# Retention attention feeding a Mish MLP on one core: first tile's chunks interleaved, four DMA transposes moved to TensorE, loads and stores reordered

## The chip, the core and the metric

The kernel runs on one core of a Trainium2 chip. A core has TensorE (PE in the profile; its weight loads are PEld), VectorE (DVE), ScalarE (ACT), GpSimd (POOL), a queue that only issues transfers (SP), and 16 DMA engines that all queues share. Each engine takes its instructions in program order and waits at the first one that is not ready. The metric is the device time of one execution in microseconds (us); lower is better.

## The reference, cut to what matters

```python
# q, k, v: (8 batches, 8 heads, 576 positions, 64), f32
scores = (1 / sqrt(64)) * q @ k^T
Dmat   = gamma[h] ** (i - j) where i >= j, else 0      # gamma = 1 - 2**(-5-h)
ret    = (scores * Dmat) @ v
x      = ret as (4608, 512)                            # 8 * 576 tokens, 8 heads * 64
h      = x @ w_in                                      # (512, 2048)
g      = h * tanh(softplus(h))                         # Mish
out    = g @ w_out                                     # (2048, 512), f32
```

## The kernel before

**Work units.** The 576 positions of a batch are cut into four chunks of 128 and one of 64; the two short ones of a pair of batches are put together. That makes 36 chunks of 128 tokens. Four chunks make a tile, so there are nine tiles, numbered t = 0 to 8. Chunks 0 to 3 are tile 0, chunks 4 to 7 tile 1, chunk 8 (a joined one) begins tile 2.

**Attention of a chunk n** has four steps, written P, T, S, O:

- P (`prep`, lines 160 to 168): DVE scales q by the decay and the softmax scale into bf16 (`qks`, line 166), GpSimd casts k (line 165) and scales v (`vs`, line 167).
- T (`step_t`, lines 170 to 181): q and k of the chunk are transposed into `qkT`, eight blocks of 128x128. For chunks 0 to 3 TensorE does it into PSUM and ACT copies it out (lines 177, 178); for all later chunks one DMA transpose on the ACT queue does it (line 180).
- S (`step_s`, lines 183 to 206): scores (`sc`, line 190), masked by DVE into `sm` (line 194), and the update of the running state k^T v (`st`, line 204).
- O (`step_o`, lines 208 to 231): state times q (line 218) and scores times v (line 223) into `ot`; DVE makes the next state copy `ssb` (line 227) and writes the chunk's columns of `xT` (line 231).

**The MLP.** `g1(t, f)` is four matmuls of 512 columns for one of 16 blocks f of the hidden width, and a Mish on ACT (line 244). `g2(t, i)` is four matmuls of the second product (line 252). Tile 0 is special: its second product is a loop over f (lines 317 to 331, "the f loop") with four accumulators, two of them in the pool of `hp`, and the attention of chunks 4 to 7 stands between its steps. Then four result tiles are copied and stored (line 333, `store` at lines 257 to 265; `res` has three buffers, so the fourth copy waits until the first store has left). Then t = 1 runs `g1(1, f)` with the attention of chunks 8 to 11 and the transposes of 9 to 12 in between and no second product; from t = 2 on each step has a `g1` and a `g2`.

**Order.** Nothing reorders instructions: the program's order is each engine's order. SP issues all loads and stores. Input buffers hold eight chunks (`io`, 8 buffers), `qks` and `vs` three, the score PSUM `sc` one. Weights come in eight pieces each through four staging buffers and are cast by GpSimd (lines 113, 115).

Of the kernel before, what the change touches and what calls it, by code (L numbers as in the profile page):

```python
# [10 lines left out]
F32 = mybir.dt.float32  # L11
BF16 = mybir.dt.bfloat16
AX = mybir.ActivationFunctionType
# [4 lines left out]
def kernel(  # L18
# [18 lines left out]
    nc = tc.nc  # L37
    B, H, S, D = q.shape
    assert (B, H, S, D) == (8, 8, 576, 64)
    P = 128  # L40
    NP = H // 2
# [4 lines left out]
    NCH = 4  # L46
# [10 lines left out]
    consts = ctx.enter_context(tc.tile_pool(name="consts", bufs=1))  # L57
# [7 lines left out]
    STG = 4  # L65
    stage = ctx.enter_context(tc.tile_pool(name="stage", bufs=STG))
    PS = bass.MemoryType.PSUM
    ps_sc = ctx.enter_context(tc.tile_pool(name="ps_sc", bufs=1, space=PS))
# [3 lines left out]
    ps_o = ctx.enter_context(tc.tile_pool(name="ps_o", bufs=2, space=PS))  # L72
# [6 lines left out]
    def load(n):  # L79
        b, c = chunks[n]  # L80
        tiles = []
        for nm, src in (("q", q), ("k", k), ("v", v)):
            t = io.tile([P, H, D], F32, name=f"{nm}raw")
            if c < 4:
                nc.sync.dma_start(  # L85
                    out=t, in_=src[b, :, ds(P * c, P), :].rearrange("h p d -> p h d"))
            else:
                for e in range(2):
                    nc.sync.dma_start(
                        out=t[ds(64 * e, 64)],  # L90
                        in_=src[b + e, :, ds(512, 64), :].rearrange("h p d -> p h d"))
            tiles.append(t)
        raw[n] = tiles
# [8 lines left out]
    def load_w(nm, i):  # L102
        t = stage.tile([P, 1024], F32, name="wst")
        if nm == "in":
            nc.sync.dma_start(out=t.rearrange("p (c f) -> p c f", c=KC), in_=w_in_r[:, :, ts(i, 256)])  # L105
        else:
            nc.sync.dma_start(out=t.rearrange("p (f d) -> p f d", f=2), in_=w_out_r[:, ts(i, 2), :])
        staged[nm, i] = t

    def cast_w(nm, i):  # L110
        t = staged.pop((nm, i))
        if nm == "in":
            nc.gpsimd.tensor_copy(w_in_t[:, :, ts(i, 256)], t.rearrange("p (c f) -> p c f", c=KC))  # L113
        else:
            nc.gpsimd.tensor_copy(w_out_t[:, ts(i, 2), :], t.rearrange("p (f d) -> p f d", f=2))
# [20 lines left out]
    gv = consts.tile([P, 5, H], F32)  # L136
    nc.scalar.activation(gq, ex, AX.Exp)
    nc.scalar.activation(gv, ex, AX.Exp, scale=-1.0)
    nc.vector.tensor_scalar(gq, gq, 1.0 / math.sqrt(D), None, op0=OP.mult)

    mask = consts.tile([P, P], F32)
# [18 lines left out]
    def prep(n):  # L160
        b, c = chunks[n]
        qr, kr, vr = raw.pop(n)
        qks = tok.tile([P, 2, H, D], BF16, name="qks")
        vs = tok.tile([P, H, D], BF16, name="vs")
        nc.gpsimd.tensor_copy(qks[:, 1], kr)  # L165
        nc.vector.tensor_tensor(qks[:, 0], qr, gq[:, c, :].unsqueeze(2).to_broadcast([P, H, D]), op=OP.mult)  # L166
        nc.gpsimd.tensor_tensor(vs, vr, gv[:, c, :].unsqueeze(2).to_broadcast([P, H, D]), op=OP.mult)  # L167
        live[n] = (qks, vs)

    def step_t(n):  # L170
        qks, vs = live[n]
        flat = qks.rearrange("p i h d -> p (i h d)")
        qk = tr.tile([P, 2, NP, P], BF16, name="qkT")
        if n < NCH:
            tp = ps_o.tile([P, 2 * NP, P], BF16, name="ops")
            for i in range(2 * NP):
                nc.tensor.transpose(tp[:, i, :], flat[:, ts(i, P)], ident)  # L177
            nc.scalar.copy(qk.rearrange("p i n t -> p (i n) t"), tp)
        else:
            nc.scalar.dma_start_transpose(out=qk.rearrange("p i n t -> p (i n) t"), in_=flat)  # L180
        live[n] = (qk, qks[:, 1], vs)

    def step_s(n):
        b, c = chunks[n]
        qk, ks, vs = live[n]
        sc = ps_sc.tile([P, 2, NP, P], F32, name="sc")
        for p in range(NP):
            for e in range(2):
                r = ds(64 * e, 64)
                nc.tensor.matmul(sc[:, e, p, :], lhsT=qk[r, 1, p, :], rhs=qk[r, 0, p, :],  # L190
                                 start=True, stop=True)
        sm = tr.tile([P, 2, NP, P], BF16, name="sm")
        m = mask if c < 4 else mask2
        nc.vector.tensor_tensor(  # L194
            sm.rearrange("p e n i -> p (e n) i"), sc.rearrange("p e n i -> p (e n) i"),
            m.unsqueeze(1).to_broadcast([P, 2 * NP, P]), op=OP.mult)
        if c < 4:
            if c == 0:
                st_ps[b] = ps_st.tile([P, NP, P], F32, name="st")
            st = st_ps[b]  # L200
            kf = ks.rearrange("p h d -> p (h d)")
            vf = vs.rearrange("p h d -> p (h d)")
            for p in range(NP):
                nc.tensor.matmul(st[:, p, :], lhsT=kf[:, ts(p, P)], rhs=vf[:, ts(p, P)],  # L204
                                 start=(c == 0 and p == 0), stop=True, skip_group_check=True)
        live[n] = (qk, sm, vs)
# [60 lines left out]

    n_chunks = len(chunks)

    def att(n, step):  # L270
        if n >= n_chunks:
            return
        if step == "P":
            prep(n)
            if n >= 2 * NCH - 1 and n + PF < n_chunks:
                load(n + PF)
        elif step == "T":
            step_t(n)
        elif step == "S":
            step_s(n)  # L280
        else:
            step_o(n)


    for n in range(NCH):
        for step in "PTSO":
            att(n, step)
    for i in range(8):
        cast_w("in", i)
        if i + STG < 8:  # L290
            load_w("in", i + STG)
        g1(0, 2 * i)
        g1(0, 2 * i + 1)
    load(4)
    att(4, "P")
    att(4, "T")
    for i in range(STG):
        load_w("out", i)
        if i % 2:
            load(4 + (i + 1) // 2)  # L300

    accs = [ps_o.tile([P, d_model], F32, name="ops") for _ in range(2)]
    accs += [ps_h.tile([P, NCH * P], F32, name="hp") for _ in range(2)]

    def more(j, n):
        cast_w("out", j)
        if j + STG < 8:
            load_w("out", j + STG)
        if j == 1:
            load(7)  # L310
        elif j == 3:
            for m in range(2 * NCH, 2 * NCH + 4):
                load(m)
        elif j in (4, 6):
            load(2 * NCH + 2 + j // 2)

    for f in range(nF):
        n, w = NCH + f // 4, f % 4
        if w == 0:
            more(f // 2, n)  # L320
            att(n, "S")
        elif w == 1:
            att(n + 1, "P")
        elif w == 2:
            more(f // 2, n)
            att(n, "O")
        else:
            att(n + 1, "T")
        for s in range(NCH):
            nc.tensor.matmul(accs[s], lhsT=gts[0][:, f, ts(s, P)], rhs=w_out_t[:, f, :],  # L330
                             start=(f == 0), stop=(f == nF - 1))
    for s in (2, 3, 0, 1):
        store(0, s, accs[s], nc.vector.tensor_copy if s % 2 else nc.scalar.copy)
    for t in range(1, nT + 1):
# [44 lines left out]
```

## Time and profile before

| what | value |
|---|---|
| median of 3 runs | 373.93 us (373.87 to 376.4) |
| the profiled execution | 374.25 us, of which the span of its instructions is 372.4 us |
| TensorE busy | 311.9 us, 84% of the span, mean granted clock 0.95 |
| DVE, ACT, POOL busy | 36%, 25%, 23% |
| longest chain, by engine | PE 66%, DMA 18%, SP queue 10% |
| longest chain, largest DMA part | `qkT<-qks` 12% |
| moved by DMA | 54.87 MB, 147 GB/s over the span |

Read it by stages: TensorE's 84% is a mean over a stretch with little idle time (from about 130 us on) and stretches ahead of it with much. The granted clock is given as a share of full speed; 0.50 is the lower of the two levels (1.2 GHz) and 1.00 the upper (2.4 GHz). The chain of waits names, from the last instruction backwards, what each piece of work waited for.

### The profile page before, as it was taken

The page shows a single profiled execution, that of the slowest core. Times are in us where ns is not written, and L with a number is a line of the kernel's source. Part 1 is how long each engine was busy: PE and PEld are TensorE (multiplying, and loading weights), DVE is VectorE, ACT ScalarE, POOL GpSimd, SP SyncE. Part 2 cuts the span into 40 slices and gives each one's busy share as a digit, 9 for nine tenths or more (in the row PEclk, how much of TensorE's full clock was granted, in tenths as well). Part 3 has the DMA queues.
Part 4 walks back from the last instruction along what each step waited for, and adds up shares of the span by engine and source line. Part 5 has one row for each costly group of instructions (what it writes and reads, how often), then busy time and mean ns, then how long its engine had stood idle before and what let it go on. Part 6 is the DMA issues. An engine that isn't in the chain of part 4 may idle for free.

```text
span 372.4 us, 5097 instructions
## 1 busy us (share of the span) xinstructions
PE 311.9 (84%) x2016; PEld 148.8 (40%) x2016; DVE 134.2 (36%) x186; ACT 93.9 (25%) x154; POOL 85.5 (23%) x100
## 2 busy tenths in 40 slices
PE   2458928744056799999999999999999999999995
PEld 1343413321023354444444444444444444444442
DVE  3542024430054535434335553433455444210021
ACT  2133600010013333232332223233222323233300
POOL 4575433221012223222222322222232210000000
PEclk9999958995569999999999999999999999999999
DMA  9999997599999828787986789899222322101022
GB/s 177 245 350 255 273 286 108 113 180 218 232 221 202 164 56 165 164 175 132 191 164 143 154 163 178 147 157 182 68 68 76 84 58 58 28 35 51 28 77 66
DMA packets 157976, 54.87 MB, mean 147 GB/s; under 512 B 147200, under 2 KB 151296, under 8 KB 157952
## 3 DMA queue, kind: packets, MB, share of 16 engines
q1 hardware_dynamic: 124160, 46.15, 58.3%
q10 hardware_dynamic: 33792, 8.39, 13.7%
q8 instruction: 16, 0.26, 0.3%
q14 instruction: 8, 0.07, 0.1%
HBM read 36.70 MB, written 9.44 MB: 124 GB/s over the span
## 4 chain that ended last, share of the span: by engine, by line
PE 66%; DMA 18%; SPq 10%; issue 3%; DVE 2%; POOL 1%; ACTq 1%; ACT 0%; DVEq 0%; POOLq 0%
PE ops L252 30%; PE hp L242 27%; DMA qkT<-qks 12%; SPq L85 9%; DMA wst<-in_moe_w_in_dram 3%; PE sc L190 3%; PE ot L223 2%; PE st L204 2%; DMA vraw<-in_v_dram 2%; PE ot L218 1%; DMA out_dram<-res 1%; DVE qks L166 1%; POOL w_in_t L113 1%; ACTq L180 1%; SPq L105 0%
## 5 line engine op out<-in xcount | busy, mean ns | idle before, releaser
L242 PE MATMUL hp<-xT,w_in_t 128*128 128x512 bf16 x576 | 150.6, 392 | 1.3 <-DVE xT L231 0.8
L244 ACT ACTIVATE gT<-hp 128x512 bf16<-128x512 f32 x144 | 85.9, 597 | 208.1 <-PE hp L242 185.7
L252 PE MATMUL ops<-w_out_t,gT 128*128 128x512 bf16 x512 | 128.8, 379 | 0.0
L242 PEld LDWEIGHTS <-w_in_t 128*128 128x128 bf16 x576 | 54.0, 100 | 63.3 <-issue 9.0
L252 PEld LDWEIGHTS <-gT 128*128 128x128 bf16 x512 | 50.1, 98 | 60.4
L259 DVE COPY res<-ops 128x512 f32<-128x512 f32 x33 | 22.8, 691 | 128.8 <-PE ops L252 104.7
L194 DVE TENSOR_TENSOR sm<-sc,mask 128x1024 bf16<-128x1024 f32 x36 | 43.9, 1219 | 51.8 <-PE sc L190 51.8
L167 POOL TENSOR_TENSOR vs<-vraw,gv 128x512 bf16<-128x512 f32 x36 | 37.8, 1050 | 106.5 <-PE ot L223 87.8
L165 POOL CAST qks<-kraw 128x512 bf16<-128x512 f32 x36 | 29.1, 807 | 101.5 <-PE st L204 60.7
L231 DVE CAST xT<-ot 128x512 bf16<-128x512 f32 x36 | 24.9, 691 | 47.7 <-PE ot L223 47.2
L190 PE MATMUL sc<-qkT 64*128 64x128 bf16 x288 | 15.6, 233 | 25.2 <-DMA qkT<-qks 20.8
L223 PE MATMUL ot<-sm,vs 128*64 128x128 bf16 x288 | 16.3, 239 | 19.9 <-DVE sm L194 19.9
L166 DVE TENSOR_TENSOR qks<-qraw,gq 128x512 bf16<-128x512 f32 x36 | 26.3, 730 | 2.9 <-DMA qraw<-in_q_dram 2.9
L190 PEld LDWEIGHTS <-qkT 64*128 64x128 bf16 x288 | 8.8, 100 | 41.0 <-DMA qkT<-qks 27.4
L227 DVE TENSOR_TENSOR ssb<-st,diag 128x512 bf16<-128x512 f32 x32 | 21.8, 680 | 0.0
L223 PEld LDWEIGHTS <-vs 128*64 128x64 bf16 x288 | 10.6, 116 | 26.2 <-issue 23.8
L204 PE MATMUL st<-vs,qks 128*128 128x128 bf16 x128 | 13.8, 235 | 0.0
L177 PE MATMUL ops<-ident,qks 128*128 128x128 bf16 x32 | 4.3, 310 | 9.6 <-DVE qks L166 9.1
L218 PEld LDWEIGHTS <-ssb 128*128 128x128 bf16 x128 | 9.6, 105 | 6.2 <-issue 0.5
L218 PE MATMUL ot<-qkT,ssb 128*128 128x128 bf16 (+1 forms) x128 | 11.8, 225 | 0.0
L330 PE MATMUL ops<-w_out_t,gT 128*128 128x512 bf16 x32 | 10.6, 417 | 0.0
L330 PE MATMUL hp<-w_out_t,gT 128*128 128x512 bf16 x32 | 10.4, 411 | 0.0
(30 smaller groups left out, 46.4 us busy)
## 6 DMA issues: line engine op xcount, KB each, us to landing
qraw<-in_q_dram SPq DMA_DIRECT2D x32, 256.0 KB, 5.1
kraw<-in_k_dram SPq DMA_DIRECT2D x32, 256.0 KB, 5.4
vraw<-in_v_dram SPq DMA_DIRECT2D x32, 256.0 KB, 5.5
out_dram<-res SPq DMA_DIRECT2D x32, 256.0 KB, 2.2
wst<-in_moe_w_in_dram SPq DMA_DIRECT2D x8, 512.0 KB, 5.7
wst<-in_moe_w_out_dram SPq DMA_DIRECT2D x8, 512.0 KB, 5.5
qraw<-in_q_dram SPq DMA_DIRECT2D x8, 128.0 KB, 5.0
kraw<-in_k_dram SPq DMA_DIRECT2D x8, 128.0 KB, 4.6
```

Of the source, the lines that this page charges most:

```text
L85: nc.sync.dma_start(out=t, in_=src[b, :, ds(P * c, P), :].rearrange("h p d -> p h d"))
L165: nc.gpsimd.tensor_copy(qks[:, 1], kr)
L166: nc.vector.tensor_tensor(qks[:, 0], qr, gq[:, c, :].unsqueeze(2).to_broadcast([P, H, D]), op=OP.mult)
L167: nc.gpsimd.tensor_tensor(vs, vr, gv[:, c, :].unsqueeze(2).to_broadcast([P, H, D]), op=OP.mult)
L190: nc.tensor.matmul(sc[:, e, p, :], lhsT=qk[r, 1, p, :], rhs=qk[r, 0, p, :], start=True, stop=True)
L194: nc.vector.tensor_tensor(sm.rearrange("p e n i -> p (e n) i"), sc.rearrange("p e n i -> p (e n) i"), m.unsqueeze(1).to_broadcast([P, 2 * ...
L218: nc.tensor.matmul(ot[:, p, ds(i0, iw)], lhsT=ssb[:, p, :], rhs=qk[:, 0, p, ds(i0, iw)], start=first, stop=False, skip_group_check=True)
L223: nc.tensor.matmul(ot[ds(64 * e, 64), p, :], lhsT=vs[:, 2 * p + e, :], rhs=sm[:, e, p, :], start=(first and p == 0), stop=True, skip_group ...
L231: nc.vector.tensor_copy(xts[t][:, :, ts(s, P)], ot)
L242: nc.tensor.matmul(hp, lhsT=w_in_t[:, c, ts(f, P)], rhs=xts[t][:, c, :], start=(c == 0), stop=(c == KC - 1))
L244: nc.scalar.activation(gts[t][:, f, :], hp, AX.Mish)
L252: nc.tensor.matmul(ops, lhsT=gts[t][:, f, ts(s, P)], rhs=w_out_t[:, f, :], start=(f == 0), stop=(f == nF - 1))
```

## The change

Five edits, all in code that sets order:

1. Tile 0: chunk n's O no longer follows its S; it comes after P and T of chunk n + 1.
2. Chunks 4 to 7 are transposed by TensorE into the score PSUM buffer and copied by ACT, as chunks 0 to 3 are (those into `ops`). From chunk 8 on it is still the DMA transpose.
3. In the f loop, P and T of chunk n stand together in its first step, S in its second, O in its fourth. Before, P and T of chunk n + 1 stood in the second and fourth step of chunk n. P and T of chunk 8 now stand behind the loop.
4. Loads go through one counter (`more_loads`). Chunks 8, 9 and 10 are loaded during the f loop; 11 and later only in the P steps of chunk 9 on, two a step, up to seven ahead. Before, chunks 8 to 14 were all issued in the f loop, ahead of tile 0's stores.
5. A Mish on one column of `pos` right after the two exponentials, so that its table is loaded there.

```diff
     nc.scalar.activation(gv, ex, AX.Exp, scale=-1.0)
+    warm = consts.tile([P, 1], F32)
+    nc.scalar.activation(warm, pos[:, 0:1], AX.Mish)
...
-        if n < NCH:
-            tp = ps_o.tile([P, 2 * NP, P], BF16, name="ops")
+        if n < 2 * NCH:
+            if n < NCH:
+                tp = ps_o.tile([P, 2 * NP, P], BF16, name="ops")
+            else:
+                tp = ps_sc.tile([P, 4 * NP, P], BF16, name="sc")[:, 0:2 * NP]
...
+    queued = [NCH]
+
+    def more_loads(upto, most):
+        while queued[0] <= min(upto, n_chunks - 1) and most:
+            load(queued[0])
+            queued[0] += 1
+            most -= 1
...
-            if n >= 2 * NCH - 1 and n + PF < n_chunks:
-                load(n + PF)
+                if n > 2 * NCH:
+                    more_loads(n + PF, 2)
...
     for n in range(NCH):
-        for step in "PTSO":
-            att(n, step)
+        att(n, "PT")
+        if n > 0:
+            att(n - 1, "O")
+        att(n, "S")
+    att(NCH - 1, "O")
...
-    load(4)
-    att(4, "P")
-    att(4, "T")
+    more_loads(4, 1)
     for i in range(STG):
         load_w("out", i)
         if i % 2:
-            load(4 + (i + 1) // 2)
+            more_loads(6, 1)
...
         if w == 0:
-            more(f // 2, n)
+            att(n, "PT")
+        elif w == 1:
             att(n, "S")
-        elif w == 1:
-            att(n + 1, "P")
-        elif w == 2:
-            more(f // 2, n)
+        elif w == 3:
             att(n, "O")
-        else:
-            att(n + 1, "T")
+        if f % 2 == 0:
+            j = f // 2
+            cast_w("out", j)
+            if j + STG < 8:
+                load_w("out", j + STG)
+            if j == 1 or j > 3 and j != 5:
+                more_loads(10, 1)
...
+    att(2 * NCH, "PT")
     for s in (2, 3, 0, 1):
         store(0, s, accs[s], nc.vector.tensor_copy if s % 2 else nc.scalar.copy)
```

DVE in tile 0, before, chunks 0 and 1 (`qks` is P, `sm` is S, `ssb` and `xT` are O):

```order
L166 TENSOR_TENSOR qks<-qraw,gq 128x512
L194 TENSOR_TENSOR sm<-sc,mask 128x1024
L227 TENSOR_TENSOR ssb<-st,diag 128x512
L231 CAST xT<-ot 128x4x128
L166 TENSOR_TENSOR qks<-qraw,gq 128x512
L194 TENSOR_TENSOR sm<-sc,mask 128x1024
```

The same place after (line numbers are those of the changed kernel):

```order
L168 TENSOR_TENSOR qks<-qraw,gq 128x512
L199 TENSOR_TENSOR sm<-sc,mask 128x1024
L168 TENSOR_TENSOR qks<-qraw,gq 128x512
L232 TENSOR_TENSOR ssb<-st,diag 128x512
L236 CAST xT<-ot 128x4x128
L199 TENSOR_TENSOR sm<-sc,mask 128x1024
```

The second chunk's q moved ahead of the first chunk's `ssb` and `xT`.

ACT from the constants to the first matmuls of t = 1, before (`ops` and `hp` in a COPY to `res` are tile 0's accumulators):

```order
L138 ACTIVATE gv<-ex 128x40
L178 COPY qkT<-ops 128x1024 x4
L244 ACT_TABLE_LOAD
L244 ACTIVATE gT<-hp 128x512 x16
L180 DMA_TRANSPOSE qkT<-qks 128x8x128 x5
L259 COPY res<-hp 128x512
L259 COPY res<-ops 128x512
L244 ACTIVATE gT<-hp 128x512
L180 DMA_TRANSPOSE qkT<-qks 128x8x128
```

The same place after:

```order
L138 ACTIVATE gv<-ex 128x40
L140 ACT_TABLE_LOAD
L140 ACTIVATE warm<-pos 128x1
L183 COPY qkT<-ops 128x1024 x4
L249 ACTIVATE gT<-hp 128x512 x16
L183 COPY qkT<-sc 128x1024 x4
L185 DMA_TRANSPOSE qkT<-qks 128x8x128
L264 COPY res<-hp 128x512
L264 COPY res<-ops 128x512
L249 ACTIVATE gT<-hp 128x512
L185 DMA_TRANSPOSE qkT<-qks 128x8x128
```

Four of the five transposes in a row became copies out of PSUM; the table load moved up. The five are chunks 4 to 8, the one behind the next Mish is chunk 9.

SP around the four stores of tile 0, before (the loads ahead are those of chunk 14):

```order
L85 DMA qraw<-in_q_dram 128x8x64
L85 DMA kraw<-in_k_dram 128x8x64
L85 DMA vraw<-in_v_dram 128x8x64
L262 DMA out_dram<-res 128x512 x4
L85 DMA qraw<-in_q_dram 128x8x64
```

After (the loads with two halves each are chunk 8, then 9 and 10):

```order
L89 DMA qraw<-in_q_dram 64x8x64 x2
L89 DMA kraw<-in_k_dram 64x8x64 x2
L89 DMA vraw<-in_v_dram 64x8x64 x2
L85 DMA qraw<-in_q_dram 128x8x64
L85 DMA kraw<-in_k_dram 128x8x64
L85 DMA vraw<-in_v_dram 128x8x64
L85 DMA qraw<-in_q_dram 128x8x64
L85 DMA kraw<-in_k_dram 128x8x64
L85 DMA vraw<-in_v_dram 128x8x64
L267 DMA out_dram<-res 128x512 x4
L85 DMA qraw<-in_q_dram 128x8x64
```

The stores moved ahead of the loads of chunks 11 to 14, twelve transfers. All that stands on SP ahead of chunk 8's loads kept its order.

## Rows read from the trace of the kernel before

**Rows 1.** Windows by stage: us, busy of each engine (instructions), clock, DMA share, GB/s.

```profile
0.00:29.51 29.51, 12.75 (x124) 9.23 (x125) 13.93 (x28) 6.97 (x8) 15.79 (x27) 1.00 1.13 259
29.51:46.01 16.50, 16.50 (x64) 6.76 (x63) 0.73 (x1) 8.96 (x15) 8.11 (x10) 1.00 1.09 260
46.01:53.16 7.15, 0.01 (x2) 0.01 (x2) 0.00 (x0) 0.60 (x1) 3.65 (x4) 0.66 1.15 271
53.16:78.35 25.19, 21.66 (x156) 10.15 (x156) 12.46 (x16) 0.17 (x1) 7.20 (x9) 0.89 0.78 152
78.35:83.17 4.82, 0.01 (x2) 0.01 (x2) 0.69 (x1) 0.90 (x2) 0.88 (x2) 0.93 1.38 142
83.17:105.71 22.54, 4.56 (x24) 2.13 (x25) 2.42 (x3) 0.60 (x1) 2.09 (x3) 0.50 1.19 224
105.71:130.29 24.58, 18.76 (x133) 8.34 (x133) 12.23 (x14) 8.25 (x14) 5.99 (x7) 0.92 1.11 193
130.29:372.40 242.11, 237.64 (x1517) 112.16 (x1516) 91.72 (x123) 67.46 (x113) 41.77 (x42) 1.00 0.53 110
```

**Rows 2.** Timeline of chunk 2 in tile 0: start, us, instruction, [idle before <-releaser].

```profile
17.19 0.68 DVE L166 TENSOR_TENSOR qks<-qraw,gq 128x512 bf16<-128x512 f32 x1
...
17.93 1.04 PE L177 MATMUL ops<-ident,qks 128*128 128x128 bf16 x8 [1.38 <-DVE qks L166]
...
19.00 1.01 ACT L178 COPY qkT<-ops 128x1024 bf16<-128x1024 bf16 x1 [5.08 <-PE ops L177]
...
20.07 0.61 PE L190 MATMUL sc<-qkT 64*128 64x128 bf16 x8 [1.10 <-ACT qkT L178]
...
20.72 1.23 DVE L194 TENSOR_TENSOR sm<-sc,mask 128x1024 bf16<-128x1024 f32 x1 [2.85 <-PE sc L190]
...
23.28 0.68 DVE L166 TENSOR_TENSOR qks<-qraw,gq 128x512 bf16<-128x512 f32 x1
```

**Rows 3.** Timeline of the f loop: last w_out loads and casts, chunk 5.

```profile
50.11 1.41 SPq L107 DMA_DIRECT2D wst<-in_moe_w_out_dram  x2
...
59.41 2.02 POOL L115 CAST w_out_t<-wst 128x1024 bf16<-128x1024 f32 x2
...
61.78 0.40 PE L190 MATMUL sc<-qkT 64*128 64x128 bf16 x8 [1.51 <-DMA qkT<-qks]
...
62.35 0.59 PE L330 MATMUL ops<-w_out_t,gT 128*128 128x512 bf16 x2
...
64.08 0.39 PE L218 MATMUL ot<-qkT,ssb 128*128 128x128 bf16 x4
...
64.85 0.69 DVE L231 CAST xT<-ot 128x512 bf16<-128x512 f32 x1 [0.20 <-PE ot L223]
```

**Rows 4.** Chain of waits: start, us, transposes of chunks 4, 6, 7 and 8.

```profile
46.20 6.92 DMA qkT<-qks
...
64.21 3.04 DMA qkT<-qks
...
69.73 3.73 DMA qkT<-qks
...
75.84 7.28 DMA qkT<-qks
```

**Rows 5.** Timeline around the four stores of tile 0.

```profile
78.18 0.58 ACT L259 COPY res<-hp 128x512 f32<-128x512 f32 x1 [31.53 <-PE hp L330]
...
99.08 5.20 SPq L262 DMA_DIRECT2D out_dram<-res  x4
103.23 0.69 DVE L259 COPY res<-ops 128x512 f32<-128x512 f32 x1 [24.15 <-DMA out_dram<-res]
...
104.60 1.37 ACTq L180 DMA_TRANSPOSE qkT<-qks  x1
...
105.71 0.64 PE L223 MATMUL ot<-sm,vs 128*64 128x128 bf16 x8 [17.98 <-DVE sm L194]
```

**Rows 6.** The page's list of DMA issues: KB each, median us to landing.

```profile
out_dram<-res SPq DMA_DIRECT2D x32, 256.0 KB, 2.2
```

More of the change, by code (lines that the diff above doesn't have):

```diff
@@ L268, with att @@
     n_chunks = len(chunks)
-    def att(n, step):
+    queued = [NCH]
[4 more added lines that the diff above has]
+            most -= 1
+    def att(n, steps):
         if n >= n_chunks:
             return
-        if step == "P":
-            prep(n)
-            if n >= 2 * NCH - 1 and n + PF < n_chunks:
-                load(n + PF)
[L277 to L280, printed above, removed]
-        else:
-            step_o(n)
-    for n in range(NCH):
-        for step in "PTSO":
-            att(n, step)
+        for step in steps:
+            if step == "P":
+                prep(n)
+                if n > 2 * NCH:
+                    more_loads(n + PF, 2)
+            else:
+                {"T": step_t, "S": step_s, "O": step_o}[step](n)
+    for n in range(NCH):
+        att(n, "PT")
[3 more added lines that the diff above has]
+    att(NCH - 1, "O")
     for i in range(8):
@@ L299 @@
         if i % 2:
-            load(4 + (i + 1) // 2)
+            more_loads(6, 1)
     accs = [ps_o.tile([P, d_model], F32, name="ops") for _ in range(2)]
     accs += [ps_h.tile([P, NCH * P], F32, name="hp") for _ in range(2)]
[L305 to L315, printed above, removed]
     for f in range(nF):
@@ L319 @@
         if w == 0:
-            more(f // 2, n)
+            att(n, "PT")
+        elif w == 1:
             att(n, "S")
-        elif w == 1:
-            att(n + 1, "P")
-        elif w == 2:
-            more(f // 2, n)
+        elif w == 3:
             att(n, "O")
-        else:
-            att(n + 1, "T")
+        if f % 2 == 0:
[5 more added lines that the diff above has]
+                more_loads(10, 1)
         for s in range(NCH):
```

## Prediction

> **What bounds the kernel now.** I read the windows by stage first, because the page's 84% for TensorE is a mean over very different stages. The last window, 242.11 us from 130.29 on, has TensorE busy for 237.64 us at clock 1.00 [rows 1]: there it is the bound, and the change touches nothing in it but the order of some loads. The 130.29 us ahead of it hold 74.3 us of TensorE work (311.9 of the page less 237.64), so the whole question is how much of the other 56 us goes. The windows show where they lie: tile 0's attention (29.51 us, of which 12.75 busy), a pause of 7.15 us before the f loop, one of 4.82 us after it, and 22.54 us with 4.56 busy at clock 0.50 [rows 1]. Then I read the chain of waits and the timeline for what ended each pause. In tile 0 every step of a chunk waits for another engine [rows 2]. The pauses around the f loop end with DMA transposes of 6.92 and 7.28 us [rows 4]. The longest pause begins with a store: DVE's fourth copy of a result tile waited 24.15 us for a `res` buffer, the four stores were issued by SP only at 99.08, and TensorE's next O waited 17.98 us for a mask product that stood behind this copy in DVE's queue [rows 5].
>
> **The change, part by part.** All sums are made against the profiled execution: a span of 372.4 us, 374.25 us with what lies around it. The median of the runs, 373.93, is 0.3 us less, which I neglect. A measurement of this kernel tells about 1%, 3.7 us, from no change.
>
> *Tile 0.* A chunk takes 6.09 us before, from one `qks` to the next (17.19 to 23.28) [rows 2]. Of these, 0.74 us go from `qks` to the transposes on TensorE, 1.07 to ACT's copy, 1.07 to the scores and 0.65 to the mask product, which takes 1.23 [rows 2]; the rest is O and its copy. After, the next `qks` stands right behind the mask product, so the period is 0.74 + 1.07 + 1.07 + 0.65 + 1.23, about 4.8 us. O runs on TensorE while ACT copies. At the upper clock it takes some 0.77 us (64.08 to 64.85) [rows 3]; at the lower one it could outlast the copy by up to 0.4 us, so a period lies between 4.8 and 5.2. O's copy fits on DVE before the next mask product. Three periods shrink, the first chunk's start and the last one's tail don't: 3 x 1.29 = 3.9 us less (2.7 to 4.2). The first product starts at 25.6 instead of 29.51. Its weights come in the same order as before and I take its 16.50 us [rows 1] as they are: it ends at 42.1.
>
> *The table load.* It goes into time in which ACT waits, both before and after: before its first copy in a chunk ACT has 5.08 us idle [rows 2]. Nothing gained, nothing lost; if this cover were gone it would cost its own length once.
>
> *The f loop.* Before, it reaches the transpose of chunk 8 at 75.84 [rows 4], 29.8 us after the first product's end at 46.01. After, each chunk runs through this chain: transposes on TensorE, estimated at 0.55 us from the 1.07 at the lower clock [rows 2]; ACT's copy with its hand-overs 1.07, under which one step of the loop (half of 62.35 to 64.08, 0.87) runs; S 0.57 (61.78 to 62.35); two steps 1.73; O 0.77 until DVE starts its copy; then on DVE 0.69 for `xT` and 0.68 for the next `qks`, under which the fourth step runs [rows 2, 3]. Sum 6.1 us, of which about 0.8 is idle TensorE. Four chunks take 24.4, plus 0.3 because the first copy stands behind the last Mish: 24.7 instead of 29.8, so 5.1 us less. With no stall at all it would be 3.2 us better still. What could hold it up are the last pieces of w_out, and they are rival B.
>
> *From chunk 8's transpose to chunk 9's.* This took 28.8 us, 75.84 to 104.60 [rows 4, 5]. It holds the stall that the moved stores end. What is late next? Two chains run in parallel. One: the transpose is issued in 1.37, ACT copies an accumulator in 0.58 [rows 5], the store of 2.2 [rows 6] frees the buffer (up to 4.2 beside loads: 99.08 to 103.23), DVE copies in 0.69 [rows 5] and makes chunk 9's `qks` in 0.68 [rows 2], with some 0.3 of hand-overs: 5.8 us, at most 7.8. The other: the transpose itself lands, S, one group of four matmuls at the lower clock (twice 0.87), and the Mish releases ACT. At its best a transpose took 3.04, with a few loads beside it 3.73, at its worst 7.28 [rows 4]. Chunks 8 to 10 are the only loads then queued, since SP stands at the stores, so I take 3.73: 3.8 + 0.6 + 1.7 + 0.1 = 6.2 us. The later chain counts: 6.2, between 5.8 and 9.7. That is 22.6 us less (19.1 to 23.0). The mask product of chunk 8 stands on DVE behind copy and `qks` as before, and now waits a microsecond or two instead of eighteen.
>
> *t = 1.* From chunk 9's transpose at 104.60 to the first scores of t = 2 at 130.29 the order on TensorE, ACT and DVE is the same. Four DMA transposes lie bare there. A period is the landing of a transpose plus about 1.8 us (S, one group, hand-overs; 0.57 + 0.87 + 0.4). Before, the four made 25.7 us, that is 4.6 us a landing. Now two loads a chunk are issued beside them instead of one. If all four landed in 3.04 it would be 19.4 us, if in 7.28, 36.3 [rows 4]. I keep 25.7: the nearest rows are these four themselves.
>
> A rule of the Trainium skill bears on this: "DMA: Bandwidth & Descriptors", section "Queues, rings and completion order", says that each DMA engine takes turns between the queues that have work for it. By that rule a transpose beside loads, however many are queued, takes at most about twice its lone time; worked out from the lone row that is an estimate of 6.1 us, and the worst case of t = 1 would be 31.6 us instead of 36.3. The trace agrees only in part: the landing of 7.28 is above twice 3.04 [rows 4].
>
> *From t = 2 on.* Loads that were issued before 99 now come later, and SP's stores stand behind some of them. Input buffers of chunks 11 to 20 are free in time, and the DMA share is 0.53 there [rows 1], so I add 0.5 us (0 to 3).
>
> Sum: -3.9 - 5.1 - 22.6 + 0 + 0.5 = -31.1; 374.25 - 31.1 = **343 us**.
>
> **The rivals.**
>
> *A. The wait moves into t = 1.* Loads of chunks 11 to 18 are now issued there, at two a chunk, in place of being done before 99. For it: in the window 83.17 to 105.71 loads alone keep the DMA engines at a share of 1.19 [rows 1], and the transpose under loads took 7.28. Price: 36.3 - 25.7 = 10.6, so 354 us. By that rule of the Trainium skill it would be 5.9 and 349 us. Against it: transposes in that stage already landed in 4.6 us on average with a share of 1.11 [rows 1]. Chance 0.15.
>
> *B. The first part runs into the weights, or doesn't shorten.* SP issues the last two pieces of w_out until 51.52 and GpSimd casts both in 2.02 [rows 3]; with the longest landing that I see, 7.28, they are usable at 60.8. The loop needs the last one in the third step of chunk 7, at about 42.1 + 3 x 6.1 + 3.1, or 63.8. So 3 us of slack. If the loads come later than that, or the chain of tile 0 doesn't close up as worked out (a load that is late for a `qks`), the 3.9 us of tile 0 are lost again: 347 us. Chance 0.12.
>
> *C. Slower, by the clock.* TensorE is granted 0.50 after its pauses [rows 1]. If tile 0's shorter waits no longer end in the upper level and the lower one held from the first product to the start of t = 2, every matmul there would take twice as long: the first product 64 x 0.43 = 27.7 instead of 16.5 (+11.2), the loop's 16 steps +13.9, the attention in it +7.5 (4 x 1.9 again), and t = 1 some 3 us a chunk (+12): 45 us, so 388. It turns the sign from 31 us on, that is if the level stays low for over two thirds of that work. Against it: the window of the first product is at 1.00, and the loop's steps ran at the upper level with gaps of 1.5 us between [rows 1, 3], longer than those I expect. Chance 0.02.
>
> **How the numbers follow.** Forecast 0.71, A 0.15, B 0.12, C 0.02. Forecast's own bounds: all transposes of t = 1 as quick as 3.04 give 6.3 less, 337; a slow chunk 8 (+3.5), late loads (+2.5) and tile 0's short end (+1.2) together 350. The range takes in B and nearly all of A: 337 to 353. Faster by over 1% holds in all cases but C, with a little left for what I haven't seen: 0.96; within 1% 0.02; slower 0.02.
>
> **What would show it.** In the profile after: `qks` of tile 0 every 4.8 us and the first `hp` matmul near 25.6; the f loop's matmuls without the 7 us pause ahead of it and done near 66; the four stores issued within 6 us of that; the first scores of t = 2 near 99; and from there about 242 us to the end. It would be wrong if transposes in t = 1 land in 7 us each (A), if an f step waits for a `w_out_t` cast (B), or if the clock is 0.50 over the f loop (C).

## The result and the profile after

The changed kernel takes 345.88 us (median of 4 runs, 344.15 to 346.68) against 374.6 us before on the same footing: a ratio of 0.922, 95% interval 0.917 to 0.927. The forecast was 343 us, its range 337 to 353. The profiled execution took 345.22 us with a span of 343.5, where the forecast's sum means a span of 341.3. One execution of e4 below, 367.85 us, ran at a lower granted clock than its others and is left out of e4's median and ratio.

The windows of the changed kernel, cut at the same events as [rows 1]: first product starts, first product ends, transpose of chunk 8 issued, transpose of chunk 9 issued, first scores of t = 2, end. The columns are those of [rows 1].

```profile
0.00:26.71 26.71, 12.54 (x125) 8.84 (x125) 15.20 (x28) 7.18 (x9) 13.70 (x25) 1.00 1.11 251
26.71:42.11 15.40, 15.13 (x66) 6.76 (x67) 0.69 (x1) 8.96 (x15) 9.44 (x10) 1.00 1.13 290
42.11:67.27 25.16, 21.23 (x185) 10.62 (x185) 13.30 (x17) 4.55 (x5) 12.13 (x14) 1.00 1.10 235
67.27:72.97 5.70, 2.30 (x12) 0.99 (x14) 1.93 (x4) 1.21 (x3) 1.65 (x2) 0.79 0.64 188
72.97:100.82 27.85, 19.93 (x142) 9.09 (x142) 12.35 (x15) 9.41 (x16) 6.98 (x8) 0.92 1.28 208
100.82:343.50 242.68, 236.17 (x1488) 112.17 (x1516) 91.94 (x123) 66.86 (x112) 41.90 (x42) 1.00 0.60 123
```

The first scores of t = 2 come at 100.82 where they came at 130.29; what follows takes 242.68 where it took 242.11. So the whole gain lies ahead of t = 2, as [rows 1] said it must. By stage:

| stretch | before | forecast | after |
|---|---|---|---|
| first product starts | 29.51 | 25.6 | 26.71 |
| first product ends | 46.01 | 42.1 | 42.11 |
| from there to chunk 8's transpose | 29.8 | 24.7 | 25.16 |
| from there to chunk 9's transpose | 28.8 | 6.2 | 5.70 |
| from there to the first scores of t = 2 | 25.7 | 25.7 | 27.85 |
| from there to the end | 242.1 | 242.6 | 242.68 |

The timeline of tile 0 after, which answers to [rows 2]: `qks` of chunks 1 to 3, a cast beside the last of them, the first product.

```profile
9.83 0.68 DVE L168 TENSOR_TENSOR qks<-qraw,gq 128x512 bf16<-128x512 f32 x1
...
14.50 1.13 DVE L168 TENSOR_TENSOR qks<-qraw,gq 128x512 bf16<-128x512 f32 x1
...
19.58 1.04 POOL L113 CAST w_in_t<-wst 128x1024 bf16<-128x1024 f32 x1 [1.04 <-DMA wst<-in_moe_w_in_dram]
19.62 1.54 DVE L168 TENSOR_TENSOR qks<-qraw,gq 128x512 bf16<-128x512 f32 x1
...
26.71 0.59 PE L247 MATMUL hp<-xT,w_in_t 128*128 128x512 bf16 x1 [0.78 <-POOL w_in_t L113]
```

The periods are 4.67 and 5.12 us against the 4.8 to 5.2 worked out, but the scaling of q itself grew from 0.68 to 1.13 and 1.54 us beside work on GpSimd. The first matmul of the product is put down to a cast of w_in; that cast and the last `xT` both ended at 26.66, and the piece that this matmul reads is the one cast from 19.58 to 20.62, so it is `xT` that it waited for.

The timeline of the f loop after, chunk 6 (TensorE transposes, ACT copies, then the scores); the last cast of a w_out piece stands in it.

```profile
54.52 0.62 PE L182 MATMUL sc<-ident,qks 128*128 128x128 bf16 x8 [0.84 <-DVE qks L168]
...
55.23 1.01 ACT L183 COPY qkT<-sc 128x1024 bf16<-128x1024 bf16 x1 [5.60 <-PE sc L182]
...
56.30 0.40 PE L195 MATMUL sc<-qkT 64*128 64x128 bf16 x8 [0.30 <-ACT qkT L183]
...
57.16 1.04 POOL L115 CAST w_out_t<-wst 128x1024 bf16<-128x1024 f32 x1 [1.08 <-DMA wst<-in_moe_w_out_dram]
...
59.97 0.95 DVE L168 TENSOR_TENSOR qks<-qraw,gq 128x512 bf16<-128x512 f32 x1
```

Where chunk 5 waited 1.51 us for its transfer [rows 3], chunk 6 now waits 0.84 and 0.30 us, for DVE and ACT. The weights are done at 58.2, ahead of the 60.8 allowed for.

The timeline around the four stores of tile 0, which answers to [rows 5]:

```profile
67.27 1.33 ACTq L185 DMA_TRANSPOSE qkT<-qks  x1
68.64 0.59 ACT L264 COPY res<-hp 128x512 f32<-128x512 f32 x1 [5.94 <-POOL qks L167]
...
69.25 3.28 SPq L267 DMA_DIRECT2D out_dram<-res  x4
...
70.45 0.53 PE L195 MATMUL sc<-qkT 64*128 64x128 bf16 x8 [3.70 <-DMA qkT<-qks]
...
71.48 0.69 DVE L264 COPY res<-ops 128x512 f32<-128x512 f32 x1 [3.77 <-DMA out_dram<-res]
...
72.83 0.60 ACT L249 ACTIVATE gT<-hp 128x512 bf16<-128x512 f32 x1 [3.12 <-remote]
72.97 1.26 ACTq L185 DMA_TRANSPOSE qkT<-qks  x1
```

The stores are issued at 69.25, not at 99.08; the fourth copy waits 3.77 us instead of 24.15, and TensorE's pause for chunk 8 is 3.70 us. The windows of t = 1 from each DMA transpose's issue to the scores that wait for it, chunks 9 to 12 (columns as in [rows 1]; the clock and the DMA share are the last but two and the last but one), first in the kernel before:

```profile
104.60:110.60 6.00, 4.17 (x16) 1.43 (x15) 2.75 (x3) 1.79 (x3) 1.04 (x1) 0.57 1.17 229
112.37:118.42 6.05, 3.03 (x21) 1.05 (x19) 2.19 (x3) 2.25 (x4) 1.04 (x1) 1.00 1.21 196
120.13:124.83 4.70, 3.14 (x24) 1.39 (x23) 2.25 (x3) 2.30 (x4) 1.04 (x1) 1.00 1.22 207
126.86:130.29 3.43, 2.92 (x23) 1.26 (x22) 1.92 (x3) 1.28 (x3) 1.04 (x1) 1.00 0.47 86
```

Then in the changed kernel:

```profile
72.97:79.03 6.06, 3.75 (x28) 1.67 (x27) 2.23 (x3) 2.25 (x4) 0.36 (x1) 0.92 1.18 238
80.80:86.95 6.15, 2.92 (x20) 1.05 (x19) 1.78 (x3) 2.25 (x4) 2.53 (x3) 1.00 1.33 215
89.46:94.62 5.16, 4.02 (x24) 1.76 (x23) 1.69 (x2) 2.25 (x4) 1.04 (x1) 0.85 1.31 188
96.71:100.82 4.11, 2.92 (x22) 1.24 (x20) 1.86 (x3) 1.93 (x4) 1.04 (x1) 1.00 1.18 163
```

One correction to the text ahead of the prediction: counted on SP's queue, chunk 15 too was loaded ahead of tile 0's stores, since chunk 8's P stood in the f loop; the three loads shown there ahead of the stores are its loads. Fifteen transfers moved behind the stores, not twelve.

### The profile page after: what moved, and what is told of

Same layout as the page of the kernel before. It is cut to its first block, busy times and chain, and to the rows that moved or that the text cites. A ratio compares the mean times of both kernels' runs of the same rounds, so it can differ in the third digit from the quotient of the medians.

```text
span 343.5 us, 5127 instructions
## 1 busy us (share of the span) xinstructions
PE 307.3 (89%) x2012; PEld 148.5 (43%) x2048; DVE 135.4 (39%) x186; ACT 98.2 (29%) x159; POOL 85.8 (25%) x100
## 4 chain that ended last, share of the span: by engine, by line
PE 75%; DMA 14%; SPq 4%; issue 2%; DVE 1%; POOL 1%; ACT 1%; ACTq 0%; POOLq 0%; DVEq 0%
PE hp L247 33%; PE ops L257 31%; DMA qkT<-qks 6%; SPq L85 4%; DMA wst<-in_moe_w_in_dram 3%; PE sc L195 3%; PE ot L228 3%; PE st L209 3%; DMA vraw<-in_v_dram 2%; DMA kraw<-in_k_dram 2%; PE ot L223 1%; ACT qkT L183 1%; DVE qks L168 1%; PE hp L331 1%; PE ops L331 1%
## 5 line engine op out<-in xcount | busy, mean ns | idle before, releaser
L247 PE MATMUL hp<-xT,w_in_t 128*128 128x512 bf16 x547 | 146.8, 389 | 2.6 <-POOL w_in_t L113 0.8
L257 PE MATMUL ops<-w_out_t,gT 128*128 128x512 bf16 x508 | 128.4, 379 | 0.3
L168 DVE TENSOR_TENSOR qks<-qraw,gq 128x512 bf16<-128x512 f32 x36 | 27.6, 766 | 5.5 <-DMA qraw<-in_q_dram 5.5
L228 PEld LDWEIGHTS <-vs 128*64 128x64 bf16 x288 | 9.8, 114 | 6.4 <-issue 4.0
L182 PEld LDWEIGHTS <-qks 128*128 128x128 bf16 x64 | 4.9, 118 | 15.9 <-DVE qks L168 14.6
L115 POOL CAST w_out_t<-wst 128x1024 bf16<-128x1024 f32 x8 | 8.5, 1065 | 5.0 <-DMA wst<-in_moe_w_out_dram 5.0
```

Source lines behind the costliest of these rows:

```text
L228: nc.tensor.matmul(ot[ds(64 * e, 64), p, :], lhsT=vs[:, 2 * p + e, :], rhs=sm[:, e, p, :], start=(first and p == 0), stop=True, skip_group ...
L247: nc.tensor.matmul(hp, lhsT=w_in_t[:, c, ts(f, P)], rhs=xts[t][:, c, :], start=(c == 0), stop=(c == KC - 1))
L257: nc.tensor.matmul(ops, lhsT=gts[t][:, f, ts(s, P)], rhs=w_out_t[:, f, :], start=(f == 0), stop=(f == nF - 1))
```

## The experiments

Each ratio is to the kernel before, run on the same chip, with its 95% interval; the changed kernel's is 0.922 (0.917 to 0.927). "Chunk 8's scores" stands for the start of its score matmuls (70.45 after).

**e1: the kernel before with edit 4 alone.**

```diff
+    queued = [2 * NCH + 3]
+    def more_loads(upto, most):
...
-            if n >= 2 * NCH - 1 and n + PF < n_chunks:
-                load(n + PF)
+            if n > 2 * NCH:
+                more_loads(n + PF, 2)
...
-            for m in range(2 * NCH, 2 * NCH + 4):
+            for m in range(2 * NCH, 2 * NCH + 3):
...
-        elif j in (4, 6):
-            load(2 * NCH + 2 + j // 2)
```

> The kernel before with edit 4 alone: chunks 8 to 10 loaded in the f loop, 11 and later two a chunk from t = 1 on, so that tile 0's stores stand ahead of those loads. Theory (the stall of 18 us behind the f loop is the stores' place on SP, whoever does the transposes): the stores go out right after their copies, near 79, chunk 9's transpose near 83 instead of 104.6, t = 1 some 2 us longer for the doubled loads: about 19 us less than before, 355 us. Rival (the stall came from the DMA transposes that share the transfer engines with the loads, and ends only when TensorE takes them): within 3 us of before, 371 to 374.

Measured: 362.89 us, 0.965 (0.958 to 0.972), between the two. The timeline at the stores, and below it the chain of waits in t = 1:

```profile
78.92 7.45 SPq L262 DMA_DIRECT2D out_dram<-res  x4
85.32 0.69 DVE L259 COPY res<-ops 128x512 f32<-128x512 f32 x1 [6.10 <-DMA out_dram<-res]
86.69 1.32 ACTq L180 DMA_TRANSPOSE qkT<-qks  x1
```

```profile
95.20 7.10 DMA qkT<-qks
...
105.37 6.56 DMA qkT<-qks
```

The theory held for the stall: chunk 9's transpose comes at 86.69 instead of 104.60, 18 us earlier (near 83 was expected; the fourth copy still waited 6.10 us for a store). It did not hold for the total. t = 1 then takes 31.7 us (86.69 to 118.39) instead of 25.7, and the rest 244.8: 9 of the 18 us are given back. The wait moves into t = 1, as rival A of the prediction has it, and more so here than in the changed kernel.

**e2: the changed kernel without edit 1** (tile 0's four steps chunk by chunk).

```diff
-        att(n, "PT")
-        if n > 0:
-            att(n - 1, "O")
-        att(n, "S")
-    att(NCH - 1, "O")
+        att(n, "PTSO")
```

> The changed kernel with tile 0 again in the order P, T, S, O chunk by chunk. Theory (tile 0 is worth 3.9 us, and nothing behind it is bound by transfers): the first product starts near 29.5 and all that follows moves by the same, 3 to 4 us slower than the changed kernel, 349 to 350. Rival (the f loop waits for the last weights and loads, so that an earlier start is lost again): within 1 us of the changed kernel, 346 to 347.

Measured: 350.06 us, 0.934 (0.927 to 0.940); the two intervals just touch, but the trace places the loss: the first product starts at 29.62 instead of 26.71, and the span is 4.4 us longer. The theory held.

**e8: the kernel before with edit 1 alone.**

```diff
-        for step in "PTSO":
-            att(n, step)
+        att(n, "P")
+        att(n, "T")
+        if n > 0:
+            att(n - 1, "O")
+        att(n, "S")
+    att(NCH - 1, "O")
```

> The kernel before with edit 1 alone. Theory (tile 0 is on the path and the 4 us stay): 3 to 4 us faster than before, 370 to 371. Rival (the stall behind the f loop ends with stores that stand behind loads, so an earlier start only makes it longer): within 1 us of before, 373 to 375.

Measured: 373.81 us, 0.993 (0.990 to 0.996), 2.5 us less than the kernel before on the same chip (376.28): between theory and rival. The first product starts at 26.33, 3.2 us earlier, and chunk 4's scores at 47.56 instead of 53.16; but chunk 8's come at 81.61 against 83.17 and the first scores of t = 2 at 128.14 against 130.29. Between, the chain of waits is DMA: transposes of 7.04, 6.79, 4.48 and 5.20 us and a load of 7.53. With transposes by DMA the f loop swallows half of what tile 0 gains: 1.6 of 3.2 us are left at chunk 8's scores.

**e3: the changed kernel without edit 5** (the table is loaded at the first Mish).

```diff
-    warm = consts.tile([P, 1], F32)
-    nc.scalar.activation(warm, pos[:, 0:1], AX.Mish)
```

> The changed kernel without edit 5, the early Mish. Theory (the table load was and is hidden): within 1 us of the changed kernel, 345 to 347; in the trace a load of 1.28 us stands on ACT between the last copy of tile 0 and the first Mish, over by the time the first product is ready. Rival (it now stands in the shortened tail of tile 0 and delays the first Mish): 1 to 1.5 us slower.

Measured: 348.2 us, 0.926 (0.921 to 0.931), which can't be told from the changed kernel. The load stands at 22.61 for 1.28 us, in time in which ACT waits; the first scores of t = 2 come at 100.79 against 100.82. So its cost is hidden in the part that edit 5 touches, and the 0.8 us of difference in the span arises only behind t = 2.

**e4: the changed kernel with DMA transposes for chunks 4 to 7** (edit 2 undone, edit 3 kept).

```diff
-        if n < 2 * NCH:
+        if n < NCH:
```

> The changed kernel with chunks 4 to 7 transposed by DMA again, at the place where TensorE now does it. Theory (the transposes on TensorE are what makes the f loop short): scores follow one step behind a transpose that lands in 3 to 7 us instead of 1.6, so each of four chunks is 2 to 5 us longer: 8 to 18 us slower than the changed kernel, 354 to 364. Rival (the new order alone makes the loop short): within 2 us of the changed kernel.

Measured: 361.2 us, 0.964 (0.955 to 0.973). Chunk 8's scores come at 84.71, 14.3 us later than 70.45, and the span is 14.5 longer. The waits of SP's queue from 40 to 90 us (line waited for, us in total, times, longest) show a second effect:

```profile
SPq L107 <- DMA qkT<-qks: 8.6, 2, 6.5
SPq L89 <- DMA qkT<-qks: 6.4, 1, 6.4
SPq L85 <- DMA qkT<-qks: 4.5, 1, 4.5
```

By this view the queue that issues the loads waited for transposes of another queue, 19.5 us in all, so that the transposes also held back loads. The order of edit 3, with only one step between T and S, needs TensorE's transposes; what edit 3 is worth by itself, TensorE's transposes in the order of before, no run shows.

**e5: the changed kernel with chunks 8 to 15 loaded ahead of the stores** (edit 4 undone).

```diff
-            if j == 1 or j > 3 and j != 5:
-                more_loads(10, 1)
+            if j in (1, 4, 5, 6, 7):
+                more_loads(15, 1)
+            elif j == 3:
+                more_loads(15, 4)
```

> The changed kernel with chunks 8 to 15 loaded ahead of tile 0's stores, as before the change; transposes of chunks 4 to 7 stay on TensorE. Theory (the place of the stores is what costs): five more loads of some 3.5 us each stand ahead of the stores, which go out near 82 instead of 69.3, and chunk 9's transpose comes near 86 instead of 73; t = 1 gets back 2 to 3 us, since its loads are already in: 8 to 12 us slower than the changed kernel, 354 to 358. Rival (with the transposes off the transfer engines the loads are through before the stores): within 2 us of the changed kernel.

Measured: 363.69 us, 0.969 (0.963 to 0.974): the direction held, the loss was larger. The timeline of SP's queue and of DVE's fourth copy:

```profile
65.03 0.98 SPq L85 DMA_DIRECT2D qraw<-in_q_dram  x1
...
71.30 0.37 SPq L85 DMA_DIRECT2D kraw<-in_k_dram  x1
...
86.35 5.36 SPq L267 DMA_DIRECT2D out_dram<-res  x4
90.66 0.69 DVE L264 COPY res<-ops 128x512 f32<-128x512 f32 x1 [22.08 <-DMA out_dram<-res]
```

The fourth copy waits 22.08 us, as it waited 24.15 before [rows 5], and chunk 9's transpose comes at 92.11 instead of 72.97. The gap from 66.0 to 71.30 is again SP waiting, 5.3 us, for chunk 8's transpose, which I had not put in. Taken together: edit 4 alone gives 3.5%, all the others without it 3.1%, both 7.8%. Without edit 4 the stall stands, only earlier (stores at 86.35 instead of 99.08); with edit 4 alone it is gone, but half of that is lost again in t = 1 and behind it.

**e6: TensorE's transposes for chunks 8 to 12 as well** (in t = 1 T stands behind O, so that the score PSUM is free).

```diff
-        if n < 2 * NCH:
+        if n <= 3 * NCH:
...
-                elif w == 1:
+                elif w == 1 and t > 1:
                     att(n + 1, "T")
                 elif w == 2:
                     att(n, "O")
+                    if t == 1:
+                        att(n + 1, "T")
```

> The changed kernel with TensorE transposes for chunks 8 to 12 as well; in t = 1 the transpose of chunk n + 1 stands behind the O of chunk n. Theory (the DMA transposes are the last wait of t = 1: five of them, 3.7 us idle ahead of chunk 8's scores and 27.9 us for four chunks whose TensorE work is some 5.5 us each): 2 us less at chunk 8 and 4 to 6 in t = 1, so 6 to 8 us faster than the changed kernel, 338 to 340. Rival (t = 1 is bound by its loads, which then end last): within 2 us of the changed kernel.

Measured: 339.86 us, 0.903 (0.899 to 0.908). Chunks 8 to 12 have their scores at 67.34, 76.47, 81.69, 86.92 and 92.16: 5.2 us a chunk from chunk 9 on, and the first scores of t = 2 come 8.7 us earlier. Of these 3.4 are given back behind them (246.04 instead of 242.68); the chain of waits there, of which the first two transposes:

```profile
110.18 6.67 DMA qkT<-qks
118.66 7.22 DMA qkT<-qks
```

The theory held: the four DMA transposes were the bound of t = 1, and the wait moves on to t = 2 in part.

**e10: e6 with the DMA transposes of t >= 2 issued one step earlier.**

```diff
                     att(n + 1, "P")
+                    if t > 1:
+                        att(n + 1, "T")
                     att(n, "S")
-                elif w == 1 and t > 1:
-                    att(n + 1, "T")
```

> The kernel with TensorE transposes up to chunk 12, and from t = 2 on the DMA transpose of chunk n + 1 issued in the first step of chunk n instead of the second. Theory (that kernel gave back 3 us of its 8.7 behind t = 1, because transposes that land in 6.7 to 7.8 us came just behind the step that needs them): issued some 1.5 us earlier they are in time, 335 to 337. Rival (ACT then waits for q and k of the chunk and holds up the Mish behind it): no faster than the kernel with transposes up to chunk 12, 340 or more.

Measured: 340.27 us, 0.902 (0.896 to 0.908), no different from e6. The part behind the first scores of t = 2 fell from 246.04 to 243.87, but those scores came at 93.73 instead of 92.16, in a part whose order the edit leaves alone. One trace each doesn't settle whether the step is worth 2 us.

**e7: the changed kernel with one load a step instead of two.**

```diff
-                    more_loads(n + PF, 2)
+                    more_loads(n + PF, 1)
```

> The changed kernel with one load a chunk instead of two from chunk 9 on. Theory (the DMA transposes of t = 1 land late because two loads a chunk are issued beside them; 27.9 us against 25.7 before): they land in some 4.5 us, t = 1 is 2 us shorter, 343 to 345, unless loads only two chunks ahead come late from t = 2 on. Rival (the landing doesn't depend on how many loads are queued): same t = 1 as the changed kernel.

Measured: 346.47 us, 0.920 (0.915 to 0.925); t = 1 takes 27.9 us, as in the changed kernel. The theory fell, because the edit didn't make what it was meant to: SP runs ahead of the engines in program order and issues the next step's load as soon as a buffer is free, so the number a step doesn't space the loads out.

**e9: only q is loaded for chunks 11 to 22** (k and v are taken from the same tile, so the output is another).

```diff
-        for nm, src in (("q", q), ("k", k), ("v", v)):
+        part = 11 <= n <= 22
+        for nm, src in (("q", q), ("k", k), ("v", v))[:1 if part else 3]:
...
-        raw[n] = tiles
+        raw[n] = tiles * 3 if part else tiles
```

> The changed kernel with only q loaded for chunks 11 to 22; their k and v are taken from the same tile, so a third of those bytes move and the output of these chunks is another one. Theory (in t = 1 the DMA transposes land late because the loads beside them use the same transfer engines): from chunk 9's transpose to the first scores of t = 2 it takes 20 to 23 us instead of 27.9, with landings of 3 to 4 us instead of 4 to 6, and the kernel is 5 to 7 us faster than the changed one, 339 to 341. Rival (a landing is that long by itself, or waits for something that isn't bytes): 27 to 28 us as in the changed kernel, 345 to 347.

Measured: 343.15 us, 0.911 (0.906 to 0.916); t = 1 takes 24.1 us. The windows from a transpose's issue to the scores, chunks 9 to 12 (columns as in [rows 1]; the last but one is the DMA share):

```profile
73.48:79.47 5.99, 4.31 (x28) 2.02 (x27) 1.75 (x3) 2.25 (x4) 1.64 (x2) 0.81 1.19 215
81.24:87.37 6.13, 2.98 (x22) 1.05 (x19) 2.19 (x3) 2.25 (x4) 1.04 (x1) 1.00 1.33 186
89.13:92.21 3.08, 3.08 (x25) 1.36 (x23) 2.20 (x3) 1.65 (x3) 1.04 (x1) 1.00 0.45 85
94.29:97.58 3.29, 2.86 (x22) 1.25 (x22) 1.88 (x3) 1.23 (x3) 1.04 (x1) 1.00 0.55 107
```

SP still issued loads without a pause until about 92 us. The two transposes beside them took 6.0 and 6.1 us, the two behind them 3.1 and 3.3: part of the expected gain is missing for that reason, and the view shows the cause side by side.

**e12: no loads at all for chunks 11 to 22** (all take chunk 10's tiles, another output).

```diff
+    kept = []
...
+        if 11 <= n <= 22:
+            raw[n] = kept
+            return
...
+        if n == 10:
+            kept.extend(tiles)
```

> The changed kernel without the loads of chunks 11 to 22, which all take chunk 10's tiles, so that in t = 1 the four DMA transposes have no load beside them; the output of these chunks is another one. Theory (a transpose beside loads lands in 4 to 6 us, one alone in some 3): all four land in 3.0 to 3.4, from chunk 9's transpose to the first scores of t = 2 it takes 19 to 21 us instead of 27.9, and the kernel is 7 to 9 us faster than the changed one, 337 to 339. Rival (a landing of some 6 us by itself, and the short ones of the run with a third of the loads came from elsewhere): 27 to 28 us.

Measured: 335.89 us, 0.893 (0.888 to 0.897). The window of t = 1:

```profile
73.40:92.51 19.11, 18.75 (x145) 8.87 (x144) 12.74 (x15) 8.83 (x16) 5.99 (x7) 0.95 0.31 63
```

It takes 19.11 us with TensorE busy for 18.75. So without loads beside them the four transposes are hidden (the median landing of the transposes issued from 72 to 95 us is 3.1 us), and of the 27.85 us of t = 1 8.7 are the price of the loads.

**e11: ACT casts the first piece of w_in instead of GpSimd.**

```diff
+        if n == 2:
+            cast_w("in", 0, nc.scalar.copy)
...
-        cast_w("in", i)
+        if i > 0:
+            cast_w("in", i)
```

> The changed kernel with the first w_in piece cast by ACT, between its copies of chunks 2 and 3, instead of by GpSimd. Theory (DVE's scaling of q took 1.54 us instead of 0.68 for chunk 3 because GpSimd worked beside it): it takes 0.7 to 0.9 and the first product starts up to 0.8 us earlier. Rival (that scaling is as long for another reason): 1.5 us again.

Measured, one run: 346.0 us. The timeline of tile 0, and the first three Mish of the first product:

```profile
14.36 1.12 DVE L168 TENSOR_TENSOR qks<-qraw,gq 128x512 bf16<-128x512 f32 x1
...
19.47 0.68 DVE L168 TENSOR_TENSOR qks<-qraw,gq 128x512 bf16<-128x512 f32 x1
...
25.69 0.59 PE L247 MATMUL hp<-xT,w_in_t 128*128 128x512 bf16 x1 [0.78 <-DVE xT L236]
...
27.60 0.60 ACT L249 ACTIVATE gT<-hp 128x512 bf16<-128x512 f32 x1 [5.31 <-PE hp L247]
29.30 0.60 ACT L249 ACTIVATE gT<-hp 128x512 bf16<-128x512 f32 x1 [1.11 <-PE hp L247]
31.01 0.60 ACT L249 ACTIVATE gT<-hp 128x512 bf16<-128x512 f32 x1 [1.11 <-PE hp L247]
```

Chunk 3's scaling is back at 0.68 us, and the first product starts at 25.69, where the forecast had it (25.6); chunk 2's, still beside GpSimd, keeps 1.12. The theory held for the scaling. The start is no measure of the edit: traces that leave the cast on GpSimd and have the same tile 0 start the product between 25.18 (e6) and 26.71. At the end of the product nothing is gained, 42.37 against 42.11, as the last section shows.

## Why the prediction was right

*Tile 0.* The period was right (4.67 and 5.12 against 4.8 to 5.2), and e2 and e8 show edit 1's worth at its place, 2.9 and 3.2 us at the first product's start against the forecast 3.9. The start was 1.1 us late because `qks` of chunks 2 and 3 was taken at its 0.68 [rows 2] and took 1.13 and 1.54; the last section shows that GpSimd's work beside it is the cause. The 16.50 us of the first product, "taken as they are", were 15.40, because the first part of it, at half rate, was shorter (last section). The end fell on the forecast to 0.01 us: two errors that cancel, and luck, since in the other traces with the same tile 0 (e3, e5, e6, e7, e9, e10, e12) the product starts at 25.2 to 26.0 and the transposes behind it at 39.6 to 42.4.

*The table load.* Nothing, as forecast, ahead of t = 2 (e3).

*The f loop.* 25.16 against 24.7. Scores stand at 43.72, 49.68, 56.30 and 62.76: periods of 6.0 to 6.6 us against the 6.1 summed from [rows 2, 3]. The longer two hold a `qks` of 1.11 and 0.95 us. That it is TensorE's transposes that bring it is shown by e4 (14.3 us lost without them) and e8. The cover that I named for the weights held: the last piece was cast 2.6 us earlier than the latest time that I allowed.

*From chunk 8's transpose to chunk 9's.* 5.70 against 6.2, and 28.8 before. That the loads ahead of the stores were the cause is shown from both sides: e1 removes the stall by that edit alone, e5 puts it back. Of the two chains that I ran against each other neither was clearly the later. The one through the store (67.27, copy 68.64, store 69.25, copy 71.48) has chunk 9's `qks` ready at 72.77; the one through the transpose and the first group of four matmuls has the Mish at 72.83, and the transpose follows at 72.97. They were forecast at 5.8 and 6.2 us.

*t = 1: the term that was mis-sized.* I kept 25.7 us and it took 27.85; this is the whole of the miss in the span (2.15 of 2.2). The step that failed is "I keep 25.7: the nearest rows are these four themselves". The windows above split the stretch. From issue to scores the four transposes made 20.18 us before and 21.48 after; the three stretches between them, from a chunk's scores to the next transpose, made 5.51 and 6.37.

So 1.30 of the 2.15 us are landings. The first two are as long as they were (6.0 to 6.2 us). The last two are longer, 5.16 and 4.11 instead of 4.70 and 3.43: beside the last one the DMA share is 1.18 where it was 0.47, so the loads, which had all but ended there before, now went on. The other 0.86 us are work between landings, which was to stay as it was. Of them 0.80 lie between chunk 10's scores and chunk 11's transpose, 2.51 us instead of 1.71: TensorE had waited 3.18 us for chunk 10's transpose, and its granted clock in these 2.51 us is 0.64 where it was 1.00. e12 and e9 show that it is loads that lengthen these transposes, e6 that the transposes are what bounds the stage.

The working had a slip as well. The stretch holds four landings but only three times the 1.8 us of other work, so a landing was 5.1 us before and not 4.6. With that the worst case is 34.5 us and not 36.3, rival A's price 8.8 us and not 10.6, and the best case 17.6 and not 19.4. Of rival A 1.3 us happened.

The rule of the Trainium skill weighed there ("DMA: Bandwidth & Descriptors", section "Queues, rings and completion order": an engine takes turns between queues) put a landing at 6.1 us at most, as an estimate. The changed kernel's t = 1, with 6.15 us at most from issue to scores, about keeps to it; e1 with 7.10 there and e6 with 7.22 in t = 2 don't, so it is no bound.

*What stays open.* In e1 t = 1 took 31.7 us and in the changed kernel 27.85 with the same order of loads and transposes in it. By the same split the landings made 23.99 us there and 21.48 here, and the stretches between 7.71 and 6.37, with a granted clock of 0.51 and 0.53 in two of e1's three. Why the landings differ no run here says. Shown is only where t = 1 ends without loads (19.11, e12), and that the number of loads a step in the program doesn't set it (e7).

*From t = 2 on.* 242.68 against 242.6.

*The others.* B didn't happen: no f step waits for a `w_out_t` cast. C didn't: the windows give 1.00 over the first product and the f loop. For the first 3 us of the product the blocks ran at half rate all the same (last section); the f loop's steps ran at the full one.

## What to carry to other kernels

In an engine's or queue's program order a transfer that nobody waits for yet stands ahead of one that an engine waits for: here fifteen early loads ahead of four stores cost 18 to 19 us (e1, e5). Moving them alone kept half of that, because t = 1 with its DMA transposes and the part behind it then took 9 us longer (e1). When one stall is removed, take the time of the next stage from rows with the load that will then lie beside it, not from the rows as they were; a DMA transpose took 3 us alone and 4 to 7 beside loads. Gains of edits to one chain of waits need not add up: 3.5% and 3.1% apart are 7.8% together, though the 1.2 points above the sum are hardly more than the three intervals allow. The version with TensorE's transposes up to chunk 12 (e6, 339.86 us) beats both kernels.

## What the runs showed of the hardware that I had not expected

*DVE beside GpSimd.* The scaling of q, a product of two operands in SBUF, takes 0.68 us alone and up to 1.54 beside a GpSimd cast, and 0.68 again when ACT makes the cast (e11). Nor does it take longer where it begins first: in e6 it began at 19.58 and took 0.68, and the two GpSimd casts that began at 19.60 took 2.55 us together instead of 2.08. The rows fit a wait until GpSimd is done: a cast that began at 19.58 and took 1.04 ends at 20.62, and 0.68 more is 21.30, where the scaling ended at 21.16. The Trainium skill, "SBUF — State Buffer", section "Who interferes with whom", says so: a DVE instruction with two inputs in SBUF and a GpSimd instruction that reads SBUF share a port, and the second waits for the whole of the first. The trace agrees to 0.14 us.

*A product that starts later can end at the same time.* The first Mish of the changed kernel's first product stand here, beside those of e11 above:

```profile
28.61 0.60 ACT L249 ACTIVATE gT<-hp 128x512 bf16<-128x512 f32 x1 [5.31 <-PE hp L247]
30.05 0.60 ACT L249 ACTIVATE gT<-hp 128x512 bf16<-128x512 f32 x1 [0.84 <-PE hp L247]
30.92 0.60 ACT L249 ACTIVATE gT<-hp 128x512 bf16<-128x512 f32 x1 [0.27 <-PE hp L247]
```

Blocks of four matmuls come every 1.71 us at first (29.30 to 31.01 in e11) and every 0.87 later: half the rate, which is that of the lower clock level, though the windows give the granted clock as 1.00 there. In the changed kernel the block of 1.44 us holds the change of rate, near 29.7, 3.0 us after the product's start; in e11 it came behind 31.01, near 31.4, 5.7 us after it. The 2.7 us more at half rate cost some 1.3 us, and that is where the 1.0 us of earlier start went. In e7 and e8 the blocks come every 0.86 to 0.87 us from the first one on. What ends the half rate is not settled by these runs.

*SP waits for transposes of ACT's queue.* The view of SP's waits has 5.3 us in e5 and three waits of 4.5 to 6.5 us in e4, in front of loads that use nothing of the transpose. The kernel before has it too: from 40 to 105 us SP waited 20.7 us for DMA transposes in three waits, the longest, 12.3 us, among chunk 8's loads. Its stores went out at 99.08, those of e5, with the same loads ahead of them, at 86.35. So a transpose beside loads is slowed by them and, as the view has it, holds the next ones back. Why SP waits there, and how much of edit 2's worth this is, no run shows.
